# Attention forward and backward tile step: score and dP chunks issued in groups of four with the 16-channel remainders in four row groups, bf16 scores, and work moved between VectorE, ScalarE and GpSimd

## The chip, the cores and the metric

The kernel runs on one core of a Trainium2 chip. The metric is device microseconds of one execution; the figure of a kernel is the median of several runs. The engines are named as the profile names them: PE is TensorE (PEld its weight loads), DVE is VectorE, ACT is ScalarE, POOL is GpSimd, SP is the engine that issues most DMAs.

## What is computed

The reference is the output of one E-Branchformer block and the gradients of all of its inputs, by `jax.vjp`. B = 2 sequences, T = 4000 tokens, D = 144 channels, K = 5 taps, all in bf16. The part that takes the time is the attention:

```python
xa = _layernorm(x, axis=-1)
qkv = jnp.einsum('btd,de->bte', xa, w_qkv)
scores = jnp.einsum('btd,bsd->bts', q, k) * D ** (-0.5)
p = _softmax(scores, axis=-1)
attn = jnp.einsum('bts,bsd->btd', p, v)
glob = jnp.einsum('btd,de->bte', attn, w_att_out)
```

Beside it stand a gated convolution branch (the "local" branch: a 144 to 288 product, GELU, a layer norm, a depthwise convolution of 5 taps, a product), a depthwise convolution over both branches, a last product, and the gradient of all of it for the incoming `grad_out`. There are nine outputs: the block's output, the gradient of x, and those of the seven weights.

## The kernel before, in words

The weights are fused first, so that keys and values are the normed input itself: a query row is `xa · (Wq Wkᵀ c)`, a score is its product with `xa`, and dP is the product of a fused gradient row with `xa` as well. T is cut into 32 tiles of 125 queries. The 144 channels don't fit the 128 rows of PE, so every product with `xa` transposed is two: one with `xaT_m` (channels 0 to 127) and one with `R`, whose rows 96 to 111 hold channels 128 to 143. `R` has 128 rows; the weights `qrr` that meet it are zero in all others.

`phase_att` runs the attention of one sequence, in 33 steps t, each cut in eight parts s (lines 902 to 954). In step t:

- `S_pair` (730): the scores of tile t in four pairs of 500-column chunks (s = 0 to 3). Each chunk is two matmuls into one PSUM bank (740 with `xaT_m`, 741 with `R`). DVE then writes the negative to `Pbuf` in bf16 and keeps the running minimum (745, 747), and ACT reads the PSUM tile once more for the exponential (748).
- `rescale` (750): after the fourth pair, the first three quarters of P are multiplied by factors that bring them to the last maximum, two on DVE (757), one on ACT (759); then a transposing DMA brings P to `PT` (760).
- `Y_half` (762): Y = P·xa of tile t−1 with a column of ones, 32 matmuls (768), then 1/rowsum (774), delta (778), the scaled rows Yn (780) and `QBs`, the scaled query and gradient rows (782).
- `dP_pair` (784): dP of tile t−1 in four pairs (s = 4 to 7; 790 with `xaT_m`, 791 with `R`), and DVE forms (dP − delta)·P into `Sbuf` in bf16 (794). It waits for delta, so for Y. A transposing DMA then makes `ST` (952).
- `Z_half` (804): Z of tile t−2 from `ST`, 32 matmuls (810); `X_group` (835): gradient rows accumulated over two tiles, 64 matmuls a step (849), added to `acc` by DVE (855).
- `jit_mm` and `jit_tr` (704, 717) make the next tile's query and gradient rows and transpose them to `qt`: slots 0 and 2 the 128 main channels, slots 1 and 3 the remainder.
- `local_units` (419): the local branch in small pieces, spread evenly over the steps.

Score and dP chunks share one PSUM pool `ps_sg` of two tiles of two banks each; everything else small goes through three tiles of `ps_w`. Within an engine the order of the instructions is fixed when the program is built, by a list scheduler: the code's order is the priority, and an instruction is placed as soon as the scheduler thinks it can run. After the 33 steps come the end of the attention and the merge (`last_tr`, `M.fill`, lines 955 to 974), then the next sequence.

Of the kernel before, what the change touches and what calls it, by code (L numbers as in the profile page):

```python
# [7 lines left out]
BF = mybir.dt.bfloat16  # L8
# [6 lines left out]
D = 144  # L15
# [321 lines left out]
def pre_pieces(k, W, b, S, pst):  # L337
# [4 lines left out]
    if True:  # L342
# [45 lines left out]
        def xat(g):  # L388
# [7 lines left out]
            nc.vector.tensor_copy(v8(S.R, 8 * g, 8)[96:112], pr[96:112, :, 0:PB])  # L396

# [21 lines left out]
def local_units(k, W, b, S, A, es, DHT, ps_w):  # L419
# [52 lines left out]
    def e_h(g):  # L472
        nc.scalar.activation(q_[:], th[:], ACT.Copy, scale=0.5, bias=0.5)
        nc.vector.tensor_tensor(hg[:], q_[:], hs[:], op=ALU.mult)
# [23 lines left out]
    def e_gn(g):  # L498
        rs, t = rsr[slot(g)], gd(g + 1)
        nc.vector.scalar_tensor_tensor(rs[:, G2:2 * G2], live["mv"][:, :, 0], -1.0, rs[:, 0:G2], op0=ALU.mult, op1=ALU.mult)  # L500
        for bi in range(G2):
            nc.scalar.activation(t[:, 0, bi, :], hg[:, bi, D:2 * D], ACT.Identity, scale=rs[:, bi:bi + 1], bias=rs[:, G2 + bi:G2 + bi + 1])
# [12 lines left out]
    def e_m(g):  # L515
        nc.scalar.activation(th[:], q_[:], ACT.Copy, scale=-1.0, bias=1.0)
        nc.vector.tensor_tensor(z_[:], th[:], hg[:], op=ALU.mult)
# [38 lines left out]
    def dgn_unit(g):  # L556
# [14 lines left out]
        for bi in range(G2):  # L571
            nc.scalar.activation(w_[:, bi, :], t[:, 0, bi, :], ACT.Identity, scale=nc1[:, bi:bi + 1], bias=c0[:, bi:bi + 1])
# [91 lines left out]
def phase_att(k, W, b, S, A, M, head=None):  # L664
# [6 lines left out]
    with ExitStack() as es:  # L671
# [16 lines left out]
        qrr = [ab.tile([PB, 2, 128], BF, name="qr%d" % i) for i in range(3)]  # L688
# [8 lines left out]
        xaTm, R, xaa = S.xaT_m, S.R, S.xa_aug  # L697
        QT, QB, RL, DL, YZ, ZN, ZT, NM, DHT = {}, {}, {}, {}, {}, {}, {}, {}, {}
        units, u0 = [], 0
# [4 lines left out]
        def jit_mm(i):  # L704
# [9 lines left out]
            nc.scalar.copy(qrr[i % 3][:, :, 96:112], pj[:].rearrange("p (a b) -> p a b", b=D)[:, :, 128:D])  # L714
            QB[i] = qb

        def jit_tr(i):
            qb = QB[i]
            pt = ps_w.tile([128, 4, 128], BF, tag="w")
            for h in range(2):  # L720
                for q, src in enumerate((qb[:, h, 0:128], qrr[i % 3][:, h, :])):
                    nc.tensor.transpose(pt[:, 2 * h + q, 0:PB], src, W.ident[0:PB, 0:PB])
# [7 lines left out]
        def S_pair(i, c2):  # L730
            qt = QT[i]
# [4 lines left out]
            ps = ps_sg.tile([PB, 2, 512], F32, tag="sg")  # L736
            for h in range(2):
                c = 2 * c2 + h
                cs = slice(c * CH, (c + 1) * CH)
                nc.tensor.matmul(ps[:, h, 0:CH], qt[:, 0, :], xaTm[:, cs], start=True, stop=False)  # L740
                nc.tensor.matmul(ps[:, h, 0:CH], qt[:, 1, :], R[:, cs], start=False, stop=True)  # L741
            src = ps[:, :, 0:CH].rearrange("p h (a b) -> p h a b", b=PB)
# [847 lines left out]
```

## Time and profile before

| | |
|---|---|
| median of 3 runs | 1458.52 us (1456.56 to 1459.54) |
| profiled execution | 1457.65 us |
| its span | 1455.9 us, so 1.75 us lie around it |
| busy in the span | PE 94%, PEld 81%, DVE 81%, ACT 59%, POOL 20% |
| PE clock granted | 0.99 on average |
| DMA | 170.37 MB, mean 117 GB/s |

The span falls into parts: a head of some 60 us, the attention of sequence 0 to about 620 us, a merge to about 765 us, the attention of sequence 1 to about 1340 us, and the end. In groups of instructions a row gives the line, the engine, the operation, the tiles and their shapes, the count, the busy time in us, the mean duration in ns, and the idle time of the engine before them with what ended it. Durations of matmuls include a modelled tail, so the pace of PE is read from the starts in the timeline.

### The profile page before, as it was taken

The page shows a single profiled execution, that of the slowest core. Times are in us where ns is not written, and L with a number is a line of the kernel's source. Part 1 is how long each engine was busy: PE and PEld are TensorE (multiplying, and loading weights), DVE is VectorE, ACT ScalarE, POOL GpSimd, SP SyncE. Part 2 cuts the span into 40 slices and gives each one's busy share as a digit, 9 for nine tenths or more (in the row PEclk, how much of TensorE's full clock was granted, in tenths as well). Part 3 has the DMA queues.
Part 4 walks back from the last instruction along what each step waited for, and adds up shares of the span by engine and source line. Part 5 has one row for each costly group of instructions (what it writes and reads, how often), then busy time and mean ns, then how long its engine had stood idle before and what let it go on. Part 6 is the DMA issues. An engine that isn't in the chain of part 4 may idle for free. (4 is left out here: it accounts for less than half of the span.)

```text
span 1455.9 us, 38963 instructions
## 1 busy us (share of the span) xinstructions
PE 1371.7 (94%) x16186; PEld 1180.2 (81%) x16186; DVE 1179.7 (81%) x2747; ACT 863.0 (59%) x1636; POOL 289.0 (20%) x515
## 2 busy tenths in 40 slices
PE   5999999999999999988887999999999999999898
PEld 3778888888888888887865888888888888888797
DVE  7799988888898988869457988888888888887754
ACT  6766666666666665525456666666666666554281
POOL 8411011111111110148212012111111111111420
PEclk9999999999999999999999999999999999999999
DMA  3586767666666666774236676666676666776712
GB/s 109 104 139 118 119 119 122 123 123 112 110 119 114 117 109 123 125 170 131 81 67 121 123 123 116 110 122 126 113 122 117 122 110 119 132 123 115 209 37 64
DMA packets 559391, 170.37 MB, mean 117 GB/s; under 512 B 542447, under 2 KB 554113, under 8 KB 559172
## 3 DMA queue, kind: packets, MB, share of 16 engines
q1 hardware_dynamic: 553578, 155.57, 58.0%
q0 software_dynamic: 5088, 12.11, 3.3%
q8 instruction: 126, 2.06, 0.6%
q14 instruction: 51, 0.42, 0.1%
q10 hardware_dynamic: 548, 0.21, 0.1%
HBM read 21.04 MB, written 14.12 MB: 24 GB/s over the span
## 5 line engine op out<-in xcount | busy, mean ns | idle before, releaser
L794 DVE SCALAR_TENSOR_TENSOR Sbuf<-ps,delta,Pbuf 125x1000 bf16<-125x1000 f32 x256 | 320.2, 1256 | 31.1 <-PE ps L791 29.0
L849 PE MATMUL X<-QBs,Sbuf 125*125 125x144 bf16 x2048 | 303.0, 226 | 6.5 <-DVE acc L855 2.7
L849 PE MATMUL X<-QBs,Pbuf 125*125 125x144 bf16 x2048 | 301.9, 226 | 0.0
L849 PEld LDWEIGHTS <-Pbuf 125*125 125x125 bf16 x2048 | 262.0, 137 | 15.2 <-issue 10.8
L849 PEld LDWEIGHTS <-Sbuf 125*125 125x125 bf16 x2048 | 261.9, 137 | 5.1
L855 DVE TENSOR_TENSOR acc<-X,acc 125x432 f32<-125x432 f32 x372 | 204.3, 552 | 36.5 <-PE X L849 35.7
L740 PE MATMUL ps<-xaT_m,qt 128*125 128x500 bf16 x512 | 193.2, 377 | 9.9 <-ACT Pbuf L748 6.7
L790 PE MATMUL ps<-xaT_m,qt 128*125 128x500 bf16 x512 | 191.8, 375 | 9.1 <-ACT Pbuf L748 6.1
L741 PE MATMUL ps<-R,qt 128*125 128x500 bf16 x512 | 192.3, 376 | 0.6 <-DVE R L357 0.4
L791 PE MATMUL ps<-R,qt 128*125 128x500 bf16 x512 | 191.0, 373 | 0.0
L768 PEld LDWEIGHTS <-PT 125*125 125x125 bf16 x2048 | 149.2, 138 | 28.2 <-DMA PT<-Pbuf 10.1
L768 PE MATMUL yz<-xa_aug,PT 125*125 125x145 bf16 x2048 | 152.4, 228 | 8.6 <-DMA PT<-Pbuf 8.5
L810 PEld LDWEIGHTS <-ST 125*125 125x125 bf16 x1984 | 143.8, 138 | 16.8
L810 PE MATMUL yz<-xa_aug,ST 125*125 125x144 bf16 x1984 | 147.7, 228 | 0.0
L745 DVE TENSOR_SCALAR_CACHE_REDUCE Pbuf<-ps 125x1000 bf16<-125x1000 f32 x64 | 76.7, 1198 | 23.7 <-PE ps L741 23.1
L595 POOL TENSOR_TENSOR A_dwc<-l_fl,A_dwc 128x512 f32<-128x512 f32 (+2 forms) x48 | 35.7, 743 | 295.9 <-ACT l_fl L594 295.9
L741 PEld LDWEIGHTS <-qt 128*125 128x125 bf16 x512 | 70.4, 137 | 28.7 <-issue 9.2
L791 PEld LDWEIGHTS <-qt 128*125 128x125 bf16 x512 | 69.6, 136 | 29.6 <-issue 9.3
L740 PEld LDWEIGHTS <-qt 128*125 128x125 bf16 x512 | 70.2, 137 | 22.2 <-issue 1.8
L790 PEld LDWEIGHTS <-qt 128*125 128x125 bf16 x512 | 69.7, 136 | 22.7 <-DVE Sbuf L794 2.1
L465 POOL TENSOR_SCALAR l_a<-l_sq 125x576 bf16<-125x576 bf16 x32 | 21.5, 671 | 299.5 <-ACT l_sq L463 260.2
L814 ACT ACTIVATE zn<-yz,rl 125x144 bf16<-125x144 f32 x64 | 24.1, 376 | 95.0 <-PE yz L810 94.9
(801 smaller groups left out, 3089.8 us busy)
## 6 DMA issues: line engine op xcount, KB each, us to landing
Yn_d<-yn SPq DMA_DIRECT2D x64, 35.2 KB
Zn_d<-zn SPq DMA_DIRECT2D x64, 35.2 KB
ug_d<-ugr SPq DMA_DIRECT2D x32, 70.3 KB
xo<-in_x_dram SPq DMA_DIRECT2D x16, 140.6 KB
out_dram<-dxo SPq DMA_DIRECT2D x16, 140.6 KB
go_h<-in_grad_out_dram POOLq DMA_DIRECT2D x4, 504.0 KB, 6.7
Zn<-Zn_d SPq DMA_DIRECT2D x4, 504.0 KB
PT<-Pbuf SPq DMA_TRANSPOSE x64
```

The lines of the kernel that those rows point to most:

```text
L595: nc.gpsimd.tensor_tensor(acc, fl[0:rows, 0:n], acc, op=ALU.add)
L740: nc.tensor.matmul(ps[:, h, 0:CH], qt[:, 0, :], xaTm[:, cs], start=True, stop=False)
L741: nc.tensor.matmul(ps[:, h, 0:CH], qt[:, 1, :], R[:, cs], start=False, stop=True)
L745: nc.vector.tensor_scalar(pdst, src, -1.0, None, op0=ALU.mult, op1=ALU.min, accum_out=nm[:, 0:1])
L768: nc.tensor.matmul(Y, PT[0:PB, j, 0:PB], xaa[:, j, 0:D + 1], start=(j == 0), stop=(j == NB - 1))
L790: nc.tensor.matmul(ps[:, h, 0:CH], qt[:, 2, :], xaTm[:, cs], start=True, stop=False)
L791: nc.tensor.matmul(ps[:, h, 0:CH], qt[:, 3, :], R[:, cs], start=False, stop=True)
L794: nc.vector.scalar_tensor_tensor(sdst, ps[:, :, 0:CH].rearrange("p h (a b) -> p h a b", b=PB), DL[i][:], psrc, op0=ALU.subtract, op1=ALU.mult)
L810: nc.tensor.matmul(Z, ST[0:PB, j, 0:PB], xaa[:, j, 0:D], start=(j == 0), stop=(j == NB - 1))
L814: nc.scalar.activation(zn[:, 0:D], Z, ACT.Copy, scale=RL.pop(i)[:])
L849: nc.tensor.matmul(X[:, jj, :], l, r, start=(n_ == 0), stop=(n_ == len(ops) - 1))
L855: nc.vector.tensor_tensor(av, X[:, 0:nj, :], av, op=ALU.add)
```

## The change

**Groups of four.** `S_pair` and `dP_pair` become one function `quad`: two score chunks of tile t and two dP chunks of tile t−1 are issued together, first the four matmuls with `xaT_m`, then the four remainders. A new tensor `XR` holds the 16 remainder channels of chunk c in rows 32·(c mod 4) to 32·(c mod 4)+15, filled by small DMAs from `R`, and `jit_tr` builds the remainder weights at the same rows. So a remainder matmul reads 16 rows, and the four of a group read four different groups of 32 rows and write four PSUM banks. A group takes both tiles of `ps_sg`. A step has four groups where it had eight pairs.

```diff
+        def quad(work, stacked=True):
+            pp = [ps_sg.tile([PB, 2, 512], F32, tag="sg", name="ps") for _ in range(len(work) // 2)]
+            for r, (i, h, c) in enumerate(work):
+                mm = nc.tensor.matmul(pp[r // 2][:, r % 2, 0:CH], QT[i][:, 3 * h, :], xaTm[:, c * CH:(c + 1) * CH], start=True, stop=False)
+            with tc.issue_after(mm.ins), tc.high_priority():
+                for r, (i, h, c) in enumerate(work):
+                    q = c % 4 if stacked else 3
+                    rs = slice(32 * q, 32 * q + DR)
+                    xr = XR[rs, (c // 4) * CH:(c // 4 + 1) * CH] if stacked else R[rs, c * CH:(c + 1) * CH]
+                    nc.tensor.matmul(pp[r // 2][:, r % 2, 0:CH], QT[i][rs, 1 + (q // 2 + h) % 2, :], xr, start=False, stop=True)
...
+            def products(q):
...
+                ps = quad(S_work(t, q) + (dP_work(t - 1, q ^ 1) if ok(t - 1) else []))
+                S_exp(t, q, ps[0])
+                if ok(t - 1):
+                    PdP(t - 1, q ^ 1, ps[1], q == 3)
```

**Scores and dP out of PSUM.** ACT takes the exponential from the bf16 scores in `Pbuf`, no longer from PSUM; the running minimum is a small operation of its own. Delta is no longer subtracted in dP: three of a step's four dP tiles are copied to `Sbuf` by ACT and multiplied there by P on DVE in bf16, the fourth is multiplied by DVE straight from PSUM. What delta did is put right later: in Z by `ty`, in X by the second half of `QBs`.

```diff
-                nc.vector.tensor_scalar(pdst, src, -1.0, nm[:, c2 - 1:c2], op0=ALU.mult, op1=ALU.min, accum_out=nm[:, c2:c2 + 1])
-            nc.scalar.activation(pdst, src, ACT.Exp, bias=nm[:, c2:c2 + 1], scale=1.0)
+            nc.vector.tensor_scalar(pdst, src, -1.0, 3.0e38, op0=ALU.mult, op1=ALU.min, accum_out=nm[:, o:o + 1])
+            if c2:
+                nc.vector.tensor_tensor(nm[:, c2:c2 + 1], nm[:, c2 - 1:c2], nm[:, o:o + 1], op=ALU.min)
+            nc.scalar.activation(pdst, pdst, ACT.Exp, bias=nm[:, c2:c2 + 1], scale=-1.0)
+
+        def PdP(i, c2, src, direct):
+            if direct:
+                nc.vector.tensor_tensor(pv(Sbuf, i % NDB, c2), src, pv(Pbuf, i % NPB, c2), op=ALU.mult)
             else:
+                nc.scalar.copy(pv(Sbuf, i % NDB, c2), src)
+                sc = Sbuf[0:PB, i % NDB, c2 * 1024:(c2 + 1) * 1024]
+                nc.vector.tensor_tensor(sc, sc, pchunk(i % NPB, c2), op=ALU.mult)
...
+            nd = small.tile([PB, 1], F32, tag="nd")
+            nc.vector.scalar_tensor_tensor(nd[:], delta[:], -1.0, rl[:], op0=ALU.mult, op1=ALU.mult)
...
-            nc.scalar.activation(QBs[:, i % NPB], qb[:], ACT.Copy, scale=rl[:])
+            nc.scalar.activation(ty[:], Y[:, 0:D], ACT.Copy, scale=nd[:])
+            nc.gpsimd.tensor_scalar(QBs[:, i % NPB, 0, :], qb[:, 0, 0:D], rl[:], 1.0, op0=ALU.mult, op1=ALU.mult)
+            nc.gpsimd.tensor_scalar(g1[:], qb[:, 1, 0:D], rl[:], 1.0, op0=ALU.mult, op1=ALU.mult)
+            nc.gpsimd.tensor_scalar(g0[:], qb[:, 0, 0:D], nd[:], 1.0, op0=ALU.mult, op1=ALU.mult)
+            nc.gpsimd.tensor_tensor(QBs[:, i % NPB, 1, :], g0[:], g1[:], op=ALU.add)
...
-            nc.scalar.activation(zn[:, 0:D], Z, ACT.Copy, scale=RL.pop(i)[:])
+            nc.vector.scalar_tensor_tensor(zn[:, 0:D], Z, RL.pop(i)[:], TY.pop(i)[:], op0=ALU.mult, op1=ALU.add)
```

**Rescaling** of P stays two quarters on DVE and one on ACT, now over whole rows of 1024 with the padding, no longer 8 pieces of 125, and it stands at the end of the step.

**Moved to GpSimd.** In the local branch `e_h`, `e_m`, `e_gn` and the rows `w_` go from ACT to POOL (one such edit for all):

```diff
     def e_h(g):
-        nc.scalar.activation(q_[:], th[:], ACT.Copy, scale=0.5, bias=0.5)
+        nc.gpsimd.tensor_scalar(q_[:], th[:], 0.5, 0.5, op0=ALU.mult, op1=ALU.add)
```

`jit_mm` no longer casts the remainder on ACT; two small POOL copies put it in four places (`rems`).

**The step's order** is written anew: group 0, the Z transposes, local units, `jit_mm`, one X group; group 1, Z, the first half of the `ST` transpose; group 2, `jit_tr`, X, local units; group 3, Y of tile t−1, local units, the rest of X, the second half of the `ST` transpose, the rescaling and the `PT` transpose. At the end of a sequence Y of the last tile comes behind the last dP groups.

PE first. Before, a pair of score chunks of one tile (`ps` the PSUM tile, `qt` the transposed rows, `xaT_m` and `R` the inputs) is followed by Y:

```order
L740 LDWEIGHTS qt_5744
L740 MATMUL ps_5964<-xaT_m_64,qt_5744 125x500
L741 LDWEIGHTS qt_5744
L741 MATMUL ps_5964<-R_65,qt_5744 125x500
L740 LDWEIGHTS qt_5744
L740 MATMUL ps_5964<-xaT_m_64,qt_5744 125x500
L741 LDWEIGHTS qt_5744
L741 MATMUL ps_5964<-R_65,qt_5744 125x500
L768 LDWEIGHTS PT_118
```

Now, in the middle of sequence 0, the end of group 0 of a step (`qt_8368` is tile t, `qt_8039` tile t−1, `ps_8519` the score tile, `ps_8520` the dP tile), and what follows it:

```order
L744 MATMUL ps_8520<-xaT_m_64,qt_8039 125x500
L750 LDWEIGHTS qt_8368
L750 MATMUL ps_8519<-XR_66,qt_8368 125x500
L750 LDWEIGHTS qt_8368
L750 MATMUL ps_8519<-XR_66,qt_8368 125x500
L750 LDWEIGHTS qt_8039
L750 MATMUL ps_8520<-XR_66,qt_8039 125x500
L750 LDWEIGHTS qt_8039
L750 MATMUL ps_8520<-XR_66,qt_8039 125x500
L854 LDWEIGHTS zn0_128
```

The remainders, which stood between the main products, now stand four in a row with nothing between them.

DVE, before, from the last score pair of a step over the first dP pair and the rescaling to the next dP pair (`f` the factors, `rl` 1/rowsum, `acc<-X` the adding of an X group):

```order
L747 TENSOR_SCALAR Pbuf,nm__14772<-ps,nm__14772 125x8x125 x2
L774 RECIPROCAL rl<-yz 125x1
L468 TENSOR_TENSOR l_z<-l_a,l_hs 125x576
L778 SCALAR_TENSOR_TENSOR dj,delta<-yz,rl,qb_12345 125x144
L794 SCALAR_TENSOR_TENSOR Sbuf<-ps,delta,Pbuf 125x8x125
L757 TENSOR_SCALAR Pbuf<-Pbuf,f 125x8x125 x2
L855 TENSOR_TENSOR acc<-X,acc 125x3x144
L794 SCALAR_TENSOR_TENSOR Sbuf<-ps,delta,Pbuf 125x8x125
```

Now, from group 3 of a step to groups 0 and 1 of the next:

```order
L770 TENSOR_SCALAR Pbuf,nm__8868<-ps 125x8x125
L778 TENSOR_TENSOR Sbuf<-ps,Pbuf 125x8x125
L772 TENSOR_TENSOR nm__8868<-nm__8868 125x1
L810 RECIPROCAL rl<-yz 125x1
L813 SCALAR_TENSOR_TENSOR dj,delta<-yz,rl,qb_123 125x144
L887 TENSOR_TENSOR acc<-X,acc 125x144
L815 SCALAR_TENSOR_TENSOR nd<-delta,rl 125x1
L887 TENSOR_TENSOR acc<-X,acc 125x3x144
L793 TENSOR_SCALAR Pbuf<-Pbuf,f 125x1024 x2
L770 TENSOR_SCALAR Pbuf,nm__9205<-ps 125x8x125
L782 TENSOR_TENSOR Sbuf<-Sbuf,Pbuf 125x1024
L770 TENSOR_SCALAR Pbuf,nm__9205<-ps 125x8x125
```

The rescaling now stands ahead of the next tile's first minimum, which frees the score tile of group 0; the first dP product of the step before stood ahead of it in the old order.

More of the change, by code (lines that the diff above doesn't have):

```diff
@@ new lines, in phase_att @@
+                rescale(t, True)
+                continue
+            if t == u0 and head is not None:
+                units += local_units(k, W, b, S, A, es_loc, DHT, ps_w)
+                n_units = len(units)
+            products(0)
+            if ok(t - 3):
+                zt_tr(t - 3)
+            loc(0.25)
+            if ok(t + 1):
+                jit_mm(t + 1)
+            loc(0.5)
+            x(1)
+            products(1)
+            for h in range(2):
+                if ok(t - 2):
+                    Z_half(t - 2, h)
```

196 lines of the change are left out of this document (99 added, 97 removed).

## Prediction, before the run

> **What bounds the kernel now.** The page comes first: busy shares, then the span in 40 slices.
>
> ```profile
> PE 1371.7 (94%) x16186; PEld 1180.2 (81%) x16186; DVE 1179.7 (81%) x2747; ACT 863.0 (59%) x1636; POOL 289.0 (20%) x515
> PE   5999999999999999988887999999999999999898
> DVE  7799988888898988869457988888888888887754
> ```
>
> PE is at nine tenths in all slices of both attention parts. DVE is close behind. The windows of the two middles (PE, PEld, DVE, ACT, POOL; clock; DMA) and, below them, the Y products alone give a step:
>
> ```profile
> 76.00:564.00 488.00, 477.63 (x5522) 408.37 (x5522) 425.80 (x920) 314.36 (x592) 61.91 (x101) 1.00 0.67 119
> 794.00:1318.00 524.00, 513.37 (x5945) 439.60 (x5946) 451.44 (x970) 328.68 (x615) 68.87 (x112) 0.99 0.67 119
> ```
>
> ```profile
> 794.00:1318.00 524.00, 67.48 (x896) 66.38 (x896) 0.99 0.67 119
> ```
>
> A step has 32 Y products, so 896 are 28 steps: 524/28 = 18.7 us a step, with PE busy 513.37/28 = 18.3, DVE 451.44/28 = 16.1, ACT 328.68/28 = 11.7, POOL 68.87/28 = 2.5. PE is the bound. How much of it is work and how much hidden waiting, the starts tell: a timeline of PE in one step (start, duration).
>
> ```profile
> 904.92 0.37 PE L740 MATMUL ps<-xaT_m,qt 128*125 128x500 bf16 x1
> 905.13 0.37 PE L741 MATMUL ps<-R,qt 128*125 128x500 bf16 x1
> 905.34 0.37 PE L740 MATMUL ps<-xaT_m,qt 128*125 128x500 bf16 x1
> ...
> 905.87 0.23 PE L849 MATMUL X<-QBs,Sbuf 125*125 125x144 bf16 x1
> 905.94 0.23 PE L849 MATMUL X<-QBs,Pbuf 125*125 125x144 bf16 x1
> ...
> 914.93 0.22 PE L722 MATMUL pt<-ident,qr 125*128 125x125 bf16 x1
> 914.98 0.22 PE L722 MATMUL pt<-ident,qb 125*128 125x125 bf16 x1
> ```
>
> A 500-column matmul takes 0.21 us of PE, one of 144 columns 0.063, one of 125 columns 0.056. A step has 32 of 500 columns, so 6.7 us; half of those, 16 × 0.21 = 3.36 us, are remainders of 16 useful rows. The other matmuls of a step, at these paces by their columns, make some 11.6 us. Together 18.4 of 18.7: PE has no slack.
>
> **The change, PE.** The 16 remainders of a step become four groups of four. Two prices are needed: leaving and entering the mode with 16 rows, and four such matmuls together. For the first there are rows near the end of the program, where a 128-row transpose and a 16-row one alternate:
>
> ```profile
> 1386.23 0.22 PE L1222 MATMUL fpt<-ident,goT 128*128 128x128 bf16 x1
> 1386.38 0.18 PE L1223 MATMUL fpt<-ident,goT 16*128 16x16 bf16 x1
> 1386.49 0.23 PE L1222 MATMUL fpt<-ident,goT 128*128 128x128 bf16 x1
> ```
>
> From the 128-column one to the 16-row one 0.15 us pass, where 0.056 would do: 0.09 for going in. Back, 16 columns take 0.11: 0.10 for going out. For the second no row of this trace shows two row groups at once. The bounds are four starting together, 0.21, and one after the other, 0.84. A group then costs 0.09 + 0.21 + 0.10 = 0.40 at best and 1.03 at worst, against 0.84 now. I take four load-and-multiply pairs started at the closest pace that the rows show for 125 columns of weights, 0.056: 0.21 + 3 × 0.056 = 0.38, so 0.57 a group. That saves 0.27 × 4 = **1.08 us a step**; the ends are +1.76 and −0.76.
>
> The Trainium skill speaks for and against here. "TensorEngine Tiling (Array Packing)", Key Properties, says that changing the tiling mode drains TensorE: the 0.15 and 0.11 above agree. "TensorE: Matmul & The Clock Gate", Part 3, Measured speedup vs the span model, gives 3.07 times for four row tiles; by it an estimated group would be 0.84/3.07 + 0.19 = 0.46, the step's saving 1.5 us and the time some 1384 us.
>
> **The change, DVE and ACT.** Rows of the groups, mean ns before the second bar:
>
> ```profile
> L794 DVE SCALAR_TENSOR_TENSOR Sbuf<-ps,delta,Pbuf 125x1000 bf16<-125x1000 f32 x256 | 320.2, 1256 | 31.1 <-PE ps L791 29.0
> L740 PE MATMUL ps<-xaT_m,qt 128*125 128x500 bf16 x512 | 193.2, 377 | 9.9 <-ACT Pbuf L748 6.7 <-ACT xaT_m L392 1.4 <-DVE Sbuf L794 0.8
> L790 PE MATMUL ps<-xaT_m,qt 128*125 128x500 bf16 x512 | 191.8, 375 | 9.1 <-ACT Pbuf L748 6.1 <-DVE Sbuf L794 2.2
> L855 DVE TENSOR_TENSOR acc<-X,acc 125x432 f32<-125x432 f32 x310 | 185.8, 602 | 21.7 <-PE X L849 20.9
> L768 PE MATMUL yz<-xa_aug,PT 125*125 125x145 bf16 x2048 | 152.4, 228 | 8.6 <-DMA PT<-Pbuf 8.5
> L745 DVE TENSOR_SCALAR_CACHE_REDUCE Pbuf<-ps 125x1000 bf16<-125x1000 f32 x64 | 76.7, 1198 | 23.7 <-PE ps L741 23.1
> L757 DVE TENSOR_SCALAR Pbuf<-Pbuf,f 125x1000 bf16<-125x1000 bf16 x128 | 57.1, 489 | 10.0 <-ACT f L753 9.9
> L778 DVE SCALAR_TENSOR_TENSOR dj<-yz,rl,qb 125x144 bf16<-125x144 f32 x64 | 23.4, 366 | 1.5
> L855 DVE TENSOR_TENSOR acc<-X,acc 125x144 f32<-125x144 f32 x62 | 18.7, 301 | 14.9 <-PE X L849 14.7
> L579 DVE TENSOR_TENSOR dhr<-l_dd,gpr 125x576 bf16<-125x576 bf16 x32 | 14.5, 454 | 0.4
> L554 DVE TENSOR_TENSOR l_dd<-dugr,l_gc 125x288 bf16<-125x288 bf16 x32 | 9.4, 294 | 0.0
> L568 DVE TENSOR_TENSOR nc<-s,rsr 125x2 f32<-125x2 f32 x32 | 5.2, 161 | 0.0
> L748 ACT ACTIVATE Pbuf<-ps,nm__6525 125x1000 bf16<-125x1000 f32 x4 | 4.4, 1104 | 1.9 <-DVE Pbuf L747 1.1 <-DVE Pbuf L745 0.8
> ```
>
> DVE, a step. Removed: 4 × 1.26 = 5.02 for dP. Added: one direct product, priced as the same shape, 1.26; three bf16 products of 1024, priced from 576 and 288 elements (0.454 and 0.294, so 0.16 for 288 more): 0.69 each, 2.08; three tiny minima at 0.16, one nd at 0.16; Z's correction, priced as `dj`, 0.37. Sum −0.67, so 15.4 of what will be some 18 us. ACT gets three copies at 1.1 (priced as L748): even if it gave up nothing it would stand at 11.7 + 3.3 = 15.0, and it gives up its four local operations, `QBs`, the cast and zn: not the bound. The rescaling's new shape I cost at nothing, its 489 ns stay; at worst it takes the 0.69 of the bf16 product, 0.4 a step more.
>
> **What is late next.** A group needs both PSUM tiles, so group 1 can't start before DVE has taken the minimum of group 0. In the order shown, ahead of that minimum stand on DVE, after group 3: its minimum 1.20, direct product 1.26, tiny minimum and reciprocal 0.16 each, `dj` 0.37, a small and a large X adding 0.30 + 0.60, nd 0.16, two rescalings 0.98. That is 5.2 us by durations, but neighbours overlap by 0.08:
>
> ```profile
> 899.84 1.25 DVE L794 SCALAR_TENSOR_TENSOR Sbuf<-ps,delta,Pbuf 125x1000 bf16<-125x1000 f32 x1
> 901.01 0.60 DVE L855 TENSOR_TENSOR acc<-X,acc 125x432 f32<-125x432 f32 x1
> ```
>
> So ten operations take 4.4, group 0's minimum 1.2 more, and its tile is free 5.7 us after group 3 ends, with 0.1 for the handing over. PE in that time: Y and X, by the order some 53 products at 0.063, 3.4 us; group 0, 0.84 + 0.57 = 1.4; then 1.3 us of small products: it wants group 1 at 6.1. Level, with 0.4 to spare. But in about half the steps pieces of the local branch stand in this stretch of DVE too; over the order's steps they add 0.5 us on average, up to 3. **I take a new wait of 0.5 us a step.** Against it goes the old wait for the exponential on the PSUM tile (L748 in the two PE rows above): 6.7 + 6.1 = 12.8 us in 64 steps, 0.2 a step, which falls away as the exponential no longer reads PSUM.
>
> Sum: 1.08 − 0.5 + 0.2 = 0.78 us a step. 61 steps have four full groups (30 in sequence 0, 31 in sequence 1): 48 us. Head and ends I cost at nothing: the last dP no longer waits for Y and `PT` (at most the 8.5 us of the row L768), but Y's store, which the merge waits for, then comes later, so as much may be lost. The transposing DMAs are off the path: `PT` is issued behind the second `ST` half and has a step until Y, and SP's share of it is short:
>
> ```profile
> L760 SPq DMA_TRANSPOSE PT<-Pbuf x64: 4700/4827/5968, 35.2 to 1336.4; - x64
> ```
>
>  Against the profiled 1457.65 the 48 us make **1410 us**; the median of the runs, 1458.52, is 0.9 higher.
>
> **Rivals.**
>
> *The groups run better than I price them and DVE keeps up.* At 0.40 to 0.46 a group the step saves 1.5 to 1.76; with 0.2 of vanished wait and half the new one, some 1.5 × 61 = 92: 1366 us. For it: nothing in the order stands between the four. Against: DVE's 15.4 of a 17 us step.
>
> *VectorE becomes the bound.* POOL gets the four local operations, `QBs` and the remainder copies: from 2.5 to some 6.5 us a step (L465's 0.67, L386's 0.46 to 0.51, L507's 0.24 and A_dwc's 0.49 are its nearest prices). And POOL and DVE can hold each other up:
>
> ```profile
> L474 DVE TENSOR_TENSOR l_hg<-l_q,l_hs x32: 439/457/877, 68.8 to 1246.8; 125x576 bf16<-125x576 bf16 x32
> ```
>
> ```profile
> L757 DVE TENSOR_SCALAR Pbuf<-Pbuf,f x128: 470/480/1418, 33.8 to 1335.8; 125x1000 bf16<-125x1000 bf16 x128
> ```
>
> ```profile
> L465 POOL TENSOR_SCALAR l_a<-l_sq x32: 667/671/674, 64.7 to 1243.7; 125x576 bf16<-125x576 bf16 x32
> ```
>
> ```profile
> L386 POOL TENSOR_SCALAR xa_aug<-x_tp_n,rstd_x,lnnm x16: 452/508/807, 678.3 to 691.3; 125x144 bf16<-125x144 bf16 x16
> ```
>
> ```profile
> L507 POOL COPY gd_rem<-gd x32: 228/236/607, 74.8 to 1263.3; 125x64 bf16<-125x64 bf16 x32
> ```
>
> ```profile
> L595 POOL TENSOR_TENSOR A_dwc<-l_fl,A_dwc 80x144 f32<-80x144 f32 x16 | 7.8, 485 | 6.3 <-ACT l_fl L594 6.3
> ```
>
> The longest of each is 0.4 to 0.9 us above its median. Nine DVE operations a step have two SBUF inputs or are rescalings; POOL busy 6.5 of 18 meets a third of them, at 0.3 each: 0.9 us. Waits on DVE for results that now come from POOL add as much. Then 15.4 + 1.8 = 17.2 with the order's uneven spread makes a step of 18.3 and 1433 us. Above 18.7 a step it ends slower. "SBUF — State Buffer" in the Trainium skill, Who interferes with whom, states such a lock between the two engines; the three maxima agree with it.
>
> *The groups don't overlap: slower.* If four 16-row matmuls run one after the other, a group costs 1.03. The step then loses 0.76, DVE has time and the new wait goes, the old 0.2 is saved: +0.56 × 61 = 34, so 1492 us. It decides from 0.84 a group. For it: no row shows two row groups together, and each has a weight load of its own.
>
> **How the numbers follow.** Forecast 0.45; better groups 0.20; VectorE 0.23, of which 0.15 faster, 0.05 the same, 0.03 slower; no overlap 0.12. A measurement of this kernel can tell 0.2%, some 3 us. So faster 0.80, same 0.05, slower 0.15. The range takes in the better groups down to a little under 1366 and the VectorE case up to 1452, and leaves out the case without overlap.
>
> **What would show it.** Starts of L750 in PE's timeline: 0.06 apart is my price, 0.21 the slower rival. Starts from the last L744 to the first L750 and back: 0.09 and 0.10 above the pace. PE's wait for L770 at the first L744 of group 1: 0.5 us a step. DVE busy 15.4 us a step; 16.5 or more, with L782 and L793 far above 0.69 and 0.49, is the VectorE rival. ST and PT must not appear among PE's waits. I am wrong if a step is above 18.4 or below 17.2 us.

## The result and the profile after

| | before | after |
|---|---|---|
| time, median (range) | 1458.64 us (1456.56 to 1459.54, 4 runs) | 1503.55 us (1499.18 to 1509.72, 4 runs) |
| ratio, 95% interval | | 1.031 (1.027 to 1.035): slower |
| span of the profiled run | 1455.9 us | 1502.8 us |

The kernel became 45 us slower, where I had forecast 48 us faster. The page after, busy times, then the slices of PE and of its granted clock:

```profile
PE 1325.1 (88%) x16190; PEld 1085.6 (72%) x16190; DVE 1136.5 (76%) x3067; ACT 910.4 (61%) x1511; POOL 548.6 (37%) x1087
PE   6878989998998888988888999988988999989798
PEclk9889999999999999999888999999999999999999
```

PE has 47 us less to do than before and the nines of its middles have become eights: it waits. To see where the time lies, I cut the program where ScalarE computes the factor f of the fourth and of the last tile of each sequence, 28 steps apart. The two stretches between them are the middles. The rows are start, duration, engine, line:

```profile
107.73 0.29 ACT L787 ACTIVATE f<-nm__1308 125x3 f32<-125x3 f32 x1
654.15 0.29 ACT L787 ACTIVATE f<-nm__10616 125x3 f32<-125x3 f32 x1
839.31 0.31 ACT L787 ACTIVATE f<-nm__13571 125x3 f32<-125x3 f32 x1
1385.42 0.29 ACT L787 ACTIVATE f<-nm__22777 125x3 f32<-125x3 f32 x1
```

Windows of these five parts (length, then busy PE, PEld, DVE, ACT, POOL; clock, DMA share, GB/s), first after and then, with before's own starts of f, before:

```profile
0.00:107.73 107.73, 80.40 (x688) 56.30 (x689) 69.50 (x199) 64.75 (x132) 62.28 (x151) 0.87 0.48 102
107.73:654.15 546.42, 494.49 (x6108) 401.85 (x6106) 437.54 (x1127) 356.10 (x573) 182.07 (x360) 0.99 0.65 115
654.15:839.31 185.16, 156.39 (x1926) 135.16 (x1923) 122.47 (x376) 92.06 (x151) 90.27 (x158) 0.88 0.50 115
839.31:1385.42 546.11, 494.37 (x6065) 401.56 (x6065) 440.50 (x1112) 349.42 (x557) 182.99 (x371) 0.99 0.64 116
1385.42:1502.80 117.38, 99.43 (x1411) 90.70 (x1408) 66.46 (x254) 48.07 (x103) 30.95 (x51) 0.96 0.44 105
```

```profile
0.00:87.54 87.54, 67.32 (x610) 50.80 (x611) 66.07 (x166) 59.18 (x129) 49.07 (x124) 0.98 0.54 115
87.54:622.10 534.56, 524.16 (x6103) 449.11 (x6102) 461.98 (x999) 337.99 (x637) 67.23 (x106) 1.00 0.66 118
622.10:806.42 184.32, 152.70 (x1926) 136.50 (x1925) 123.97 (x353) 87.12 (x154) 69.89 (x117) 0.95 0.49 113
806.42:1334.93 528.51, 520.19 (x6064) 446.02 (x6063) 457.50 (x977) 331.04 (x620) 74.36 (x122) 1.00 0.68 120
1334.93:1455.90 120.97, 107.36 (x1490) 97.72 (x1488) 70.17 (x258) 47.68 (x104) 28.48 (x46) 0.96 0.43 107
```

So the 46.9 us are: the start +20.2, the two middles +11.9 and +17.6, the merge between them +0.8, the end −3.6. In the middles, 56 steps, PE is busy 988.9 us instead of 1044.4, but idle 103.7 instead of 18.7: 55.5 us of work saved, 85.0 us of waiting added. The saving itself came as hoped; one group in PE's timeline:

```profile
913.73 1.01 PE L744 MATMUL ps<-xaT_m,qt 128*125 128x500 bf16 x4
914.68 0.43 PE L750 MATMUL ps<-XR,qt 16*125 16x500 bf16 x4
915.04 0.85 PE L804 MATMUL yz<-xa_aug,PT 125*125 125x145 bf16 x10
```

Four mains (the matmuls with `xaT_m`) at 0.21 need 0.84 and the remainders begin after 0.95, so 0.11 for the change of mode. All four remainders together take 0.43, no longer than one of them by itself, and the next matmul starts 0.36 after the first. Beyond its mains a group costs 0.47 us. The largest waits of PE and some of DVE's, over the whole program, are (waiter, releaser: us in all, times, longest):

```profile
PE ps L744 <- DVE Pbuf L770: 62.8, 66, 2.2
PE X L881 <- DVE acc L887: 9.6, 10, 2.0
```

```profile
DVE Pbuf L770 <- PE ps L750: 76.6, 97, 4.4
DVE acc L887 <- PE X L881: 62.3, 66, 5.9
DVE Pbuf L793 <- ACT f L787: 23.4, 37, 2.3
DVE l_z L470 <- POOL l_a L467: 18.9, 20, 5.5
```

PE waits for DVE and DVE for PE, ScalarE and GpSimd; nobody is busy all the time (DVE 878 of 1092 us in the middles, 15.7 a step). Within the two middles PE's first wait is 56.4 of the 62.8 us, and by the trace 48.5 of these stand where the prediction looked for it, at group 1, for the minimum of group 0. Two theories came out of this. **A**: a group takes both PSUM tiles, so PE cannot run ahead of DVE. **B**: DVE stands in its order behind results that now come from GpSimd. Further ones (**D**: DVE's queue sets the step; **E**: several chains through the engines do) came up as these failed.

### The profile page after: what moved, and what is told of

Its sections match the earlier page's. It is cut to its first block, busy times and chain, and to the rows that moved or that the text cites. A ratio compares the mean times of both kernels' runs of the same rounds, so it can differ in the third digit from the quotient of the medians.

```text
span 1502.8 us, 39968 instructions
## 1 busy us (share of the span) xinstructions
PE 1325.1 (88%) x16190; PEld 1085.6 (72%) x16190; DVE 1136.5 (76%) x3067; ACT 910.4 (61%) x1511; POOL 548.6 (37%) x1087
## 5 line engine op out<-in xcount | busy, mean ns | idle before, releaser
L770 DVE TENSOR_SCALAR_CACHE_REDUCE Pbuf<-ps 125x1000 bf16<-125x1000 f32 x256 | 306.1, 1196 | 77.4 <-PE ps L750 76.6
L744 PE MATMUL ps<-xaT_m,qt 128*125 128x500 bf16 x1024 | 276.6, 383 | 69.8 <-DVE Pbuf L770 62.8
L881 PEld LDWEIGHTS <-Sbuf 125*125 125x125 bf16 x2048 | 266.5, 139 | 12.5 <-issue 12.0
L780 ACT CAST Sbuf<-ps 125x1000 bf16<-125x1000 f32 x189 | 188.0, 995 | 75.2 <-PE ps L750 74.8
L744 PEld LDWEIGHTS <-qt 128*125 128x125 bf16 x1024 | 127.5, 139 | 113.9 <-issue 79.2
L782 DVE TENSOR_TENSOR Sbuf<-Sbuf,Pbuf 125x1024 bf16<-125x1024 bf16 x189 | 132.1, 699 | 19.7 <-ACT Sbuf L780 18.4
L750 PE MATMUL ps<-XR,qt 16*125 16x500 bf16 x1016 | 113.9, 427 | 0.0
L750 PEld LDWEIGHTS <-qt 16*125 16x125 bf16 x1024 | 37.1, 129 | 103.0 <-issue 103.0
L793 DVE TENSOR_SCALAR Pbuf<-Pbuf,f 125x1024 bf16<-125x1024 bf16 x128 | 65.0, 539 | 24.4 <-ACT f L787 23.4
L778 DVE TENSOR_TENSOR Sbuf<-ps,Pbuf 125x1000 bf16<-125x1000 f32 x67 | 80.2, 1196 | 0.5 <-PE ps L750 0.3
L795 ACT ACTIVATE Pbuf<-Pbuf,f 125x1024 bf16<-125x1024 bf16 x64 | 73.4, 1147 | 1.7
```

Of the source, the lines that this page charges most:

```text
L744: mm = nc.tensor.matmul(pp[r // 2][:, r % 2, 0:CH], QT[i][:, 3 * h, :], xaTm[:, c * CH:(c + 1) * CH], start=True, stop=False)
L750: nc.tensor.matmul(pp[r // 2][:, r % 2, 0:CH], QT[i][rs, 1 + (q // 2 + h) % 2, :], xr, start=False, stop=True)
L770: nc.vector.tensor_scalar(pdst, src, -1.0, 3.0e38, op0=ALU.mult, op1=ALU.min, accum_out=nm[:, o:o + 1])
L778: nc.vector.tensor_tensor(pv(Sbuf, i % NDB, c2), src, pv(Pbuf, i % NPB, c2), op=ALU.mult)
L780: nc.scalar.copy(pv(Sbuf, i % NDB, c2), src)
L782: nc.vector.tensor_tensor(sc, sc, pchunk(i % NPB, c2), op=ALU.mult)
```

## The experiments

All times are medians of 4 to 10 runs with the ratio to before and its interval. "Middles" is the length of the two middles together, cut as above, then PE busy and PE idle in them, from the windows of each kernel. These windows are of one profiled execution each; z_split's took 1527.1 us, 9.7 above its median. Between fl2 and after, whose times are the same, the middles differ by 8 us, so less than that says nothing. The times alone don't tell min_first, no_direct, fl2 and full_pairs from after: the differences are up to 6 us and the intervals overlap.

| kernel | us | ratio | middles | PE busy | PE idle |
|---|---|---|---|---|---|
| before | 1458.6 | | 1063.1 | 1044.4 | 18.7 |
| after | 1503.6 | 1.027–1.035 | 1092.5 | 988.9 | 103.7 |
| min_first | 1497.3 | 1.022–1.030 | 1083.4 | 990.6 | 92.8 |
| z_split | 1517.4 | 1.038–1.046 | 1104.4 | 995.6 | 108.8 |
| act_back | 1490.3 | 1.020–1.025 | 1078.3 | 985.9 | 92.4 |
| no_direct | 1499.3 | 1.026–1.034 | 1082.7 | 991.8 | 91.0 |
| no_rescale | 1494.2 | 1.023–1.029 | 1081.7 | 991.5 | 90.2 |
| fl2 | 1503.7 | 1.029–1.035 | 1084.9 | 982.7 | 102.2 |
| head_pool | 1493.0 | 1.022–1.030 | 1093.5 | 989.0 | 104.4 |
| one_group | 1552.2 | 1.062–1.068 | 1128.2 | 1106.6 | 21.6 |
| full_rows | 1515.6 | 1.037–1.043 | 1105.1 | 1052.7 | 52.3 |
| pairs | 1525.8 | 1.045–1.051 | 1110.7 | 1076.9 | 33.8 |
| full_pairs | 1502.7 | 1.026–1.032 | 1100.0 | 1055.1 | 44.9 |
| rows_alone | 1515.0 | 1.037–1.043 | 1109.1 | 1003.1 | 106.0 |
| combo | 1468.0 | 1.005–1.012 | 1066.6 | 985.8 | 80.7 |
| combo_fp | 1473.1 | 1.007–1.011 | 1080.1 | 1050.1 | 30.0 |
| combo_nd | 1448.1 | 0.991–0.994 | 1046.0 | 981.9 | 64.1 |
| combo_nd_fp | 1460.8 | 1.001–1.003 | 1071.0 | 1047.9 | 23.1 |
| combo_m | 1455.8 | 0.997–1.000 | 1052.7 | 985.8 | 67.0 |

### Single waits: min_first, z_split, act_back

min_first:
```diff
             if t < NB:
-                rescale(t, True)
+                PEND.append((t, rescale(t)))
...
-                S_exp(t, q, ps[0])
+                mn = S_exp(t, q, ps[0])
+                if PEND:
+                    with tc.issue_after(mn.ins):
+                        rescale_p(*PEND.pop())
```
Here rescale gives back f alone and rescale_p does the rest of it, so ScalarE's rescaling and the transposing DMA of P come later too.

> Kernel after, with the two rescalings of a tile on VectorE moved behind the next tile's first minimum instead of ahead of it; nothing else moves on VectorE. Theory A (a group takes both PSUM tiles, so TensorE stands until VectorE has come to the minimum of group 0, behind the queue of the step before): TensorE's wait for that minimum at group 1, 62.8 us in 66 waits, falls below 20, since two rescalings, 0.9 us, no longer stand ahead of it, and the time falls by 30 to 45 us, to 1459 to 1474. Theory B (GpSimd: VectorE stands in its order behind results that now come from GpSimd): VectorE's queue is as long as before, the wait comes back elsewhere, the time is within 10 us of 1503.6.

z_split:
```diff
+            if ok(t - 2):
+                Z_half(t - 2, 0)
             products(1)
-            for h in range(2):
-                if ok(t - 2):
-                    Z_half(t - 2, h)
+            if ok(t - 2):
+                Z_half(t - 2, 1)
```


> Kernel after, with the first half of a step's Z products, 16 x 0.0625 = 1.0 us of TensorE, moved from behind group 1 to ahead of it. Theory A: that is the work TensorE lacks between group 0 and group 1; the wait for the minimum at group 1 falls from 62.8 to under 20 us, and as nothing was short behind group 1 the time falls by 30 to 60 us, to 1444 to 1474. Theory B, and the rival that VectorE's whole step is the limit: the wait moves to another group, the time is within 10 us of 1503.6.

act_back (one of the four):
```diff
-        nc.gpsimd.tensor_scalar(q_[:], th[:], 0.5, 0.5, op0=ALU.mult, op1=ALU.add)
+        nc.scalar.activation(q_[:], th[:], ACT.Copy, scale=0.5, bias=0.5)
```


> Kernel after, with the four operations of the local branch (L475, L504, L518, L574) back on ScalarE as in the kernel before; QBs and the remainder copies stay on GpSimd. Theory B: VectorE's waits for GpSimd (l_z, l_hg, rsr, l_dd: 53 us in all) and the contention between the two mostly go, and with them most of TensorE's new waits: the time falls by 30 to 50 us, to 1454 to 1474. Theory A: GpSimd matters little, the time is within 10 us of 1503.6, and the wait at group 1 stays above 50 us.

Measured: −6.3, +13.8 and −13.2 us against after. None of the three does what its theory said. z_split is the telling one; three of the largest of PE's waits there are

```profile
PE X L881 <- ACT zt L856: 23.3, 16, 2.2
PE ps L744 <- DVE Pbuf L770: 16.3, 23, 1.6
PE pj L709 <- ACT zt L856: 11.4, 12, 2.4
```

The wait at the groups fell from 62.8 to 16.3 us as asked, and PE is idle 108.8 us all the same: it now stands at other places, mostly for ScalarE's copy of zt. So where PE stands is not what makes it stand. act_back's gain is clear of the scatter. The four operations take a little longer on GpSimd in after than on ScalarE in before: l_w 504 and 499 ns, l_q 697 and 687, gd 546 and 504, l_th 861 and 689, together 8.8 us over the whole program. Whether act_back gains by this work or by the passing on and the queue, no run separates.

### DVE's load: no_direct, no_rescale

```diff
-                    PdP(t - 1, q ^ 1, ps[1], q == 3)
+                    PdP(t - 1, q ^ 1, ps[1], False)
```


> Kernel after, with the one dP product of a step that reads PSUM on VectorE (1.2 us) made like the others: copied by ScalarE (1.0), then multiplied as bf16 (0.7). VectorE has 0.5 us a step less, ScalarE 1.0 more (13.6 of 19.5). Theory D: VectorE's queue sets the step, 0.5 less gives 20 to 30 us: 1474 to 1484. Theory A: the tile of group 3 is free earlier, by 1.2 us, but the wait stands at group 1: 1493 to 1504.

no_rescale:
```diff
-                elif c2 < 2:
-                    nc.vector.tensor_scalar(p_, p_, f[:, c2:c2 + 1], None, op0=ALU.mult)
-                else:
+                elif c2 == 2:
```


> Kernel after, without the two rescalings of a tile on VectorE (0.98 us a step); so the first two chunks of P keep their own maxima and the output isn't the reference's. Order and all else as after. Theory D: every microsecond off VectorE's queue comes back whole: 0.98 x 61 = 60 us, 1444. Theory A: these two stand ahead of the minimum of group 0, so the wait at group 1 (1.04 us a step) goes, with the other waits left as they are: 1445 to 1460 too; what tells the two apart is which waits remain: by A those at group 1 fall below 0.2 us a step and the X products keep theirs, by D both shrink alike. If neither (min_first gained 6 us only by moving them): within 15 us of 1503.6.

−4.2 us, within the scatter, and −9.4. Nearly a microsecond a step off DVE's queue gives a sixth of what theory D asked for; D falls as it stands.

### The start: head_pool

GpSimd's timeline after, 33 to 61 us, and then before, 33 to 39 us (in brackets: idle time ahead and what ended it):

```profile
33.77 0.54 POOL L685 MEMSET Sbuf<- 125x288 bf16 x1
54.36 0.83 POOL L725 COPY qr<-qb 125x64 bf16<-125x64 bf16 x2 [20.04 <-ACT qb L715]
55.18 5.57 POOL L261 TENSOR_SCALAR sr<-two,cols 128x16 bf16<-128x16 bf16 x20
```

```profile
32.64 0.55 POOL L683 MEMSET Sbuf<- 125x288 bf16 x1
33.09 5.50 POOL L261 TENSOR_SCALAR sr<-two,cols 128x16 bf16<-128x16 bf16 x20
```

The remainder copy of tile 2, new on GpSimd, stands in its queue and waits 20.04 us for a copy that ScalarE makes (qb); behind it stand 20 us of constants that the kernel before began at 33.

```diff
-                rems(nc.gpsimd.tensor_copy, i, h)
+                rems(nc.scalar.copy if head is not None and i < 4 else nc.gpsimd.tensor_copy, i, h)
...
+            if head is not None and i == 0:
+                nc.vector.tensor_scalar(QBs[:, i, 0, :], qb[:, 0, 0:D], rl[:], None, op0=ALU.mult)
...
```


> Kernel after, with what GpSimd has to do for the first tiles of sequence 0 taken off its queue: the remainder copies of tiles 2 and 3 on ScalarE, QBs of tile 0 on VectorE (three operations). In the profile after, GpSimd stands from 34.3 to 54.4 us at the remainder copy of tile 2, with the constants of the convolution (L261 to L303) queued behind it; before, these ran from 33.2 to 52. Theory: this is why the fourth rescaling comes at 107.7 us instead of 87.5. Then the constants run from 33 us again and 12 to 20 us go: 1484 to 1492. Rival, that the half clock at the start (31 us of it before 107.7, against 3) and the new order are the cause: within 5 of 1503.6.

The constants run from 35 us again, the first part is 98.4 us instead of 107.7, the time 10.5 us less: a little under the range. The nine kernels of after's kind without this edit (16-row remainders in after's order) reach the fourth tile at 107.2 to 113.6 us, the four with it at 98.4 to 101.0. So about half of the start's loss is this queue.

### The parts of the change: one_group, full_rows, pairs, full_pairs, rows_alone

one_group passes stacked=False; pairs calls quad twice:
```diff
-                ps = quad(S_work(t, q) + (dP_work(t - 1, q ^ 1) if ok(t - 1) else []))
+                ps = quad(S_work(t, q)) + (quad(dP_work(t - 1, q ^ 1)) if ok(t - 1) else [])
```


> Kernel after, with all four remainders of a group on the same 16 rows, so that they run one after the other; order, engines and tiles as in after. A group of remainders then takes 4 x 0.21 + 0.19 = 1.03 us instead of 0.46. If TensorE's work sets the step: 4 x 0.57 x 61 = 139 us more, 1643. If the step is set by VectorE's queue and TensorE waits 2 us a step anyway: at most 139 - 2 x 61 = 17 us more, 1520. Theory A by itself, with a wait of 1 us a step at group 1 that the longer groups don't shorten (they stand ahead of the minimum, not beside it): about 1600.

> Kernel after, with scores and dP as two groups of two matmuls and two row groups each, one behind the other; TensorE's order is otherwise nearly that of after, and a pair needs one PSUM tile instead of both. TensorE has more to do: a group of four took 0.46 us beyond its mains, a group of two by estimate 0.38, so 1.2 us more a step. Theory A (both tiles are taken at once): the waits fall from 2.5 us a step to under 1, so more than the added work comes back, step 18.7 to 19.3, time 1470 to 1490. Theory D (VectorE's queue sets the step and tiles are not the point): the step stays 19.5 and the time within 10 us of 1503.6. If TensorE is the bound: step 20.5, 1560.

full_rows (full_pairs is both):
```diff
-                    nc.tensor.matmul(pp[r // 2][:, r % 2, 0:CH], QT[i][rs, 1 + (q // 2 + h) % 2, :], xr, start=False, stop=True)
+                    nc.tensor.matmul(pp[r // 2][:, r % 2, 0:CH], QT[i][:, 1 + h, :], R[:, c * CH:(c + 1) * CH], start=False, stop=True)
```


> Kernel after without row groups: the remainders are matmuls of 128 rows from R as in the kernel before (no XR, one remainder copy a chunk kind), all else, the groups' order, engines and tiles, as in after. TensorE has 1.44 us a step more than in after and no change of mode. If the rest of the change is what costs, its chain sets the step at 19.4 or more and the added work fills waits of 2.5 us: within 15 of 1503.6. If the groups' remainders are what costs (mode changes, the clock): the step is that of before, 19.0, plus the 20 us of the start: 1475 to 1482. The half clock in the two middles (27 us in after, none in before): gone if matmuls of 16 rows bring it on, there if waits do.

> Kernel full_rows (no row groups; after's order and engines) with the group taken apart into a score pair and a dP pair, so that each needs one PSUM tile, as in the kernel before. It is the missing corner beside after (row groups, four at a time), pairs (row groups, two) and full_rows (none, four). Theory A (both tiles taken at once): the waits fall from 1.25 us a step to some 0.5 and the step from 19.7 to 19.0 or less: 1465 to 1480 with the 20 us of the start. Theory D2 (a chain through all engines in the new order sets some 19.4 a step, whoever takes the tiles): the step stays at 19.4 to 19.7, 1500 to 1515.

rows_alone is the kernel before with XR, the spread remainders and these groups (dP likewise at s = 4 and 6):
```diff
-                if s < 4 and ok(t):
-                    S_pair(t, s)
...
+                elif s in (0, 2) and ok(t):
+                    for n_, src in enumerate(quad(S_work(t, s) + S_work(t, s + 1))):
+                        S_exp(t, s + n_, src)
```


> Kernel before with the row groups alone: the copy XR, the remainders spread over four row groups, and groups of four made of two score chunks or of two dP chunks of one tile, at the places where the first of the two stood. The order of the step, the exponential from PSUM, dP with delta from PSUM, and all work of ScalarE and GpSimd are as before (the remainder copies on ScalarE). Measured in after, a group of four saves 0.36 us against four remainders of 128 rows, so 1.44 us a step. If the rest of the change is what costs: 1459 - (0.5 to 1.44) x 61, 1371 to 1428. If it is the groups themselves (both PSUM tiles taken at once, work handed to VectorE in lumps): waits come here too and the time is 1455 to 1500.

The windows' sums over the two middles (length, PE busy first), of one_group, full_rows, full_pairs and rows_alone in this order:

```profile
sum 1128.20, PE 1106.58 PEld 859.22 DVE 887.65 ACT 709.99 POOL 366.83; mean PE 553.29 PEld 429.61 DVE 443.82 ACT 355.00 POOL 183.41
```
```profile
sum 1105.06, PE 1052.73 PEld 898.55 DVE 884.65 ACT 706.47 POOL 359.16; mean PE 526.37 PEld 449.27 DVE 442.33 ACT 353.23 POOL 179.58
```
```profile
sum 1099.97, PE 1055.12 PEld 895.99 DVE 888.15 ACT 710.21 POOL 369.43; mean PE 527.56 PEld 448.00 DVE 444.08 ACT 355.11 POOL 184.71
```
```profile
sum 1109.11, PE 1003.13 PEld 804.36 DVE 920.78 ACT 676.83 POOL 143.25; mean PE 501.57 PEld 402.18 DVE 460.39 ACT 338.42 POOL 71.62
```

Four readings. The row groups do save PE work: 1052.7 to 988.9, 1.14 us a step, full_rows against after. But the middles shorten by only 12.5 us of these 63.9; the rest is more idle time, 103.7 against 52.3. Second, full_pairs has before's matmuls, one PSUM tile at a time, and still has 36.9 us more in the middles than before (26.1 of idle PE, 10.8 of busy): the new order and the moves between the engines cost that by themselves. Third, taking both tiles costs little there: full_rows against full_pairs, 5.1 us in the middles. The times differ by 12.9; in the profiled executions another 5.7 lie in the merge. With z_split this speaks against A as the main cause in after; with the row groups themselves no run separates it, as pairs changes PE's work as well. In the order of before the groups do cost more than they save: rows_alone, where four score chunks make a group and the exponential still reads PSUM, has lost all that PE saved (41.2 us less busy, 87.3 more idle),

```profile
L744 PE MATMUL ps<-xaT_m,qt 128*125 128x500 bf16 x1024 | 295.5, 380 | 98.5 <-ACT Pbuf L769 71.4 <-DVE Sbuf L808 23.2 <-ACT xaT_m L392 1.3
```

94.6 us over the whole program of waiting at the groups, for exponentials and products. Whether it is the two tiles or the work handed over in lumps is not separated there. Fourth, in one_group PE is idle 21.6 us, as in before: given enough work, PE is the bound again, at 1128 us: 117.7 us more work than in after, 82.1 us less waiting. pairs waits little (33.8 us), but with the mode changed for eight groups a step PE is busy 21.8 us longer than in full_pairs without row groups.

### Cutting several links: combo, combo_fp, combo_nd, combo_nd_fp, combo_m

The chain of waits that ended last shows what a step of after runs through (start, us, what). It can be followed back to 1307 us only, so this is a step near the end of sequence 1, from one minimum to that of the next step:

```profile
1317.54 1.20 DVE Pbuf L770 x2
...
1320.82 0.92 POOL l_w L574 x2
1321.76 0.37 DVE l_dd L580
...
1323.01 1.12 DVE Pbuf L770 x2
...
1327.32 0.95 issue
1328.27 0.97 ACT Sbuf L780
...
1331.87 1.28 POOL A_dwc L597
...
1336.30 1.58 PE yz L842 x25
...
1338.63 0.85 PE ps L744 x4
1339.48 0.41 PE ps L750 x4
1339.89 1.20 DVE Pbuf L770 x2
```

22.35 us in this step, longer than the mean of 19.5, through DVE, GpSimd, DVE, ScalarE, GpSimd, ScalarE and PE, of which PE has some 5 us by the chain's rows. That is theory E. In before the chain of the last step lies on PE alone, from 1317.7 to 1336.4 us; rows of it:

```profile
1316.46 0.84 DVE Pbuf L757 x2
1318.25 0.75 PE X L849 x12
...
1335.33 0.75 PE X L849 x12
```

PE's share of the chain, as far as it goes back within the second middle, shows the same over longer stretches: before 86% (20 us); after 25% (78 us), no_direct 32% (417 us), no_rescale 33% (the whole middle, 534 us), with DVE, ScalarE and GpSimd having most of the rest; full_pairs 72% (192 us); combo_nd 65% (31 us); combo_nd_fp 85% (129 us). The last two are kernels of the next experiment. combo cuts four links: act_back, min_first, head_pool, and

```diff
-    fl = pl.tile([128, 512], F32, name="l_fl")
+    flr = [pl.tile([128, 512], F32, name="l_fl%d" % i) for i in range(2)]
```


> Kernel after with the buffer l_fl of the local branch doubled, nothing else: the fourth cut of combo by itself. If the cuts of combo simply add, it brings what combo (-35.6 us) has beyond act_back, min_first and head_pool (-30.0): -6 us, 1498. If combo was more than its parts: nothing, 1500 to 1507.

> Kernel after with four links of the chain shortened at once: the local branch's four operations on ScalarE (act_back, -13 us), the rescalings behind the first minimum (min_first, -6), GpSimd freed at the start (head_pool, -10), and the buffer l_fl doubled, so that ScalarE doesn't stand at it for GpSimd's addition (in after 13.5 us of ScalarE's waits in the first middle). If the gains add up: 1472 to 1476 and some 5 us for l_fl, 1468. If each single cut only uncovered the next link of a chain that goes through all four engines, together they give more than their sum: below 1460. If ScalarE, 14 to 14.5 us a step, becomes the late one: 1480 to 1490.

combo_fp and combo_nd_fp take the row groups out of combo and combo_nd, as in full_pairs; combo_nd adds no_direct; combo_m moves L518 back to GpSimd.

> Kernel full_pairs with the four cuts of combo (local operations on ScalarE, rescalings behind the first minimum, GpSimd free at the start, l_fl doubled). Combo with row groups ran at 1468. If TensorE's work is the bound once the waits are gone (17.74 + 0.73 + 0.5 = 18.97 a step, and a start as in combo): 1455 to 1465. If the row groups in combo are worth what they save TensorE, 1.7 us a step with their changes of mode: this is 60 us or more slower than combo, 1530.

> Kernel combo with the dP product from PSUM made by ScalarE's copy and a bf16 product too: VectorE 0.5 us a step less, ScalarE 1.0 more, 15 of 19. If VectorE's queue still holds the chain: 10 to 25 us less than combo, 1443 to 1458, level with the kernel before or faster. If the chain has gone over to ScalarE: 1468 to 1490.

> Kernel combo_nd (1448) without row groups: 128-row remainders, score and dP as two pairs, as in full_pairs. With full rows TensorE has 17.75 + 0.75 us of work and gaps a step, 1.7 more than with row groups. Theory E (chains through several engines are as long as TensorE's work; row groups pay as far as these are cut): in after the row groups brought nothing against full_pairs (1503.6 to 1502.7), in combo 5 us (1468 to 1473), and here 20 to 30 us: 1468 to 1478, TensorE being the bound. Rival (row groups pay nothing in any of these, since the chain sets the step in both): within 8 us of 1448.

> Kernel combo_nd with one of the four local operations, 1 - q of L518, on GpSimd again: nobody waits for it in the chain of the step, and ScalarE, at 14.9 of 18.7 us, loses some 0.5 us a step, while GpSimd goes from 4.7 to 5.5. If ScalarE's queue is what is left: 10 to 20 us less than combo_nd, 1428 to 1438. If VectorE's and TensorE's are, or GpSimd holds VectorE up: 1445 to 1455.

combo gains 35.6 us against after, its four parts by themselves 6.3 + 13.2 + 10.5 − 0.1 = 29.9: about the sum, so the doubled buffer did nothing and the stronger form of E is not shown there. no_direct, however, is worth 4.2 us in after (within the scatter) and 19.8 in combo. combo_nd is 0.8% faster than before (ratio 0.992, 0.991 to 0.994). The sums over the middles, of combo_nd and combo_nd_fp:

```profile
sum 1045.96, PE 981.90 PEld 796.22 DVE 846.82 ACT 836.50 POOL 262.93; mean PE 490.95 PEld 398.11 DVE 423.41 ACT 418.25 POOL 131.46
```
```profile
sum 1070.95, PE 1047.88 PEld 891.73 DVE 852.36 ACT 834.83 POOL 256.71; mean PE 523.94 PEld 445.87 DVE 426.18 ACT 417.42 POOL 128.36
```

What the row groups are worth in the middles grows as the chain is cut: full_pairs to after 7.4 us, combo_fp to combo 13.5, combo_nd_fp to combo_nd 25.0, of 66 us that they take off PE each time; in times −0.9, 5.2 and 12.6. Each step of this is near the 8 us of scatter; the rise from the first to the last, 17.6 us in the middles and 13.5 in the times, is more. Without them PE is idle 23 us, as before: there PE is the bound. combo_m says that what is left is not simply ScalarE's load: 0.3 us a step off it made it 7.7 us slower; that the GpSimd link is back is the likely reason, not a tested one. The kernels with row groups reach the fourth tile later than those without (100.0 us in combo, 92.5 in combo_fp; 101.0 in combo_nd, 92.1 in combo_nd_fp), which takes back 7.5 and 8.9 us. Part of it is the clock: in this first part it was granted at 0.97 and 0.95 with row groups and at 1.00 without, some 3 and 5 us of PE's time. The rest was not tried.

## Why the prediction was wrong

- **The groups: right in the main.** Priced 0.57 us, measured 0.47 beyond the mains. The parts were off both ways: the four remainders start 0.003 apart by the trace, where I had 0.06, and if one takes 0.21 as before, the change of mode costs 0.11 going in and 0.15 going out, where I had read 0.09 and 0.10. Priced 1.08 us a step, measured 1.14 of PE's busy time (full_rows to after); by the starts it is 4 × 0.37 = 1.5. By the Trainium skill's 3.07 times for four row tiles ("TensorE: Matmul & The Clock Gate", Part 3, Measured speedup vs the span model) I had an estimate of 0.46 a group: the trace's 0.47 agrees with it.
- **The loads: right.** DVE 15.7 us a step (15.4), ScalarE 12.6 (up to 15), GpSimd 6.5 (6.5), L782 0.70 (0.69). The rescaling takes 0.54 instead of 0.49, 0.1 a step.
- **"I take a new wait of 0.5 us a step": the step that failed.** At that place the middles have 48.5 us of it, 0.9 a step. Far more, it was the only wait I added. PE's idle time in the middles grew by 85.0 us, 1.5 a step, where my terms came to 0.3 (0.5 less 0.2). I compared DVE's load with the step (15.4 of 18), which says that DVE is no bottleneck; true and beside the point. In after the step is a round through several queues in order (PE has 25% of the chain there and 86% in before), and I added up one link of it. full_pairs shows that the order and the moves alone cost 37 us in the middles; the cuts in combo_nd_fp give 29 of them back, with PE's work nearly the same (1047.9 for 1055.1).
- **"Head and ends I cost at nothing (8.5 us)": wrong by 20.2 us at the start.** I noted the copies on GpSimd and did not ask what stands behind them in its queue. head_pool gives about half of it back.
- **The rivals.** "The groups don't overlap" is refuted by the timeline, and one_group at 1552 shows what it costs. "VectorE becomes the bound" named the right parties, GpSimd's results and DVE's order, by the wrong mechanism: not load and contention (DVE 80% busy) but standing in line. Its price, 18.3 a step, was under the measured 19.5. Of the rows under it, only L474, L757 and L507 have a longest 0.4 to 0.9 us above the median; L465 has 0.00 and L386 0.30.
- **The bounds.** I wrote "wrong if a step is above 18.4": it is 1092.5/56 = 19.5. Before it is 1063.1/56 = 19.0, where the window I had cut gave 18.7. ST and PT are not among PE's waits in the middles, as forecast.

Not settled: how the 37 us divide between the new order and the moves to other engines; and the clock, which I had not priced. In the first part it was granted at 0.87 instead of 0.98, some 12 us of PE's time, and in the middles at 0.99 instead of 1.00, some 10 us in all (20 us at half the clock; the 27 in the expectation of full_rows is too much), of which waits absorb a part. As that expectation asked, it goes with the 16-row matmuls. By the clock's records none of the five kernels without them (before, full_rows, full_pairs, combo_fp, combo_nd_fp, with PE idle 19 to 52 us) was granted less than the full clock anywhere in the middles. All fourteen kernels with them were, for between 3 us (rows_alone, one_group) and 31 us (z_split) at half of it. What in them brings it on was not tried; at the start waiting has a part in it, as head_pool's first part had 0.93. The slowdown does not need it: full_pairs has the full clock in the middles and the 36.9 us all the same. How much of after's own 45 us it makes is open.

## What to carry over

When an engine that was 98% busy gets work taken off, the next bound need not be another engine's load: follow the chain of one step through every queue, with the passing on, and add that up before and after the change. Ask of each operation that is moved what stands behind it in the queue it joins, at the start of the program too. A wait that goes when filler is put in its place, with the time unchanged or worse, was a symptom; an improvement that brings nothing can be worth its price once the links around it are cut.

## What the hardware showed

```profile
L750 PE MATMUL ps<-XR,qt 16*125 16x500 bf16 x1016 | 113.9, 427 | 0.0
```

Four 16-row matmuls in four row groups, 500 columns each and a weight load each, show 0.43 us together and 0.43 for one alone (the mean above, 427 ns): they start practically at once, 0.003 apart, where I had priced 0.06 between them. All fourteen kernels with 16-row matmuls had stretches of half clock in the middles, the five without had none. A bf16 product of two SBUF operands took 0.70 us (mean of L782) where the one that reads PSUM took 1.20 (L778), so moving dP's read of PSUM to ScalarE (1.0 us) takes 0.5 us off DVE; what that brought was within the scatter in after and 19.8 us in combo.
